# Loading the output projection in rows of 16, 8 and 4 KB, with attention outputs spread to match by mask products

## The chip, the cores and the metric

The kernel runs on one core of one Trainium2 chip. The metric is device time in microseconds (us) of that core, median over runs. Repeats of one kernel on one chip lie within about 0.5 us of each other.

PE is the matmul engine, DVE the vector engine, ACT the scalar engine, SP the engine that issues the loads. A load is one DMA instruction; 16 DMA engines work on it, each moving *packets*, here one contiguous run of bytes into one partition of SBUF, the core's on-chip memory, which has 128 partitions. A load *lands* when its bytes have arrived; each DMA engine reports the landing of its own share. The *cast* is the last arithmetic step, just before the store of the result.

## The reference, cut to what matters

```python
# one query token; 32 heads, 8 K/V groups of 4 heads, 65,536 keys, head size 128, bf16
xn = layernorm(x)
q  = (xn @ wq).reshape(32, 128)
o  = softmax(q @ K.T / sqrt(128)) @ V            # per head; K and V are 128 MiB each
out = x + o.reshape(4096) @ wo + ffn(xn)         # wo: 4096 x 512, 4 MiB
```

Every byte of K and V is used once, so 280.5 MB have to come in. wo is 1.5% of that, but it comes last.

## The kernel before

K comes in chunks of 4 MB (32 KB to a partition), V in chunks of 4 or 8 MB, all from one queue. PE transposes K, computes scores, and multiplies by V. wo has room only when the K buffers are free for good, so it is loaded last, behind the last half of V. The output of a head lies as a column: `oT_all[d, h]`, with the head's dimension d on the partitions.

A row of wo is 512 numbers, 1 KB. Four consecutive rows are put into one partition, so that a packet is 4 KB; the outputs must then be rearranged so that partition p holds the outputs for its four rows. That is done by 16 small matmuls with strided columns of the identity. Only the last group, whose outputs come last, keeps rows of 1 KB and needs no rearranging.

```python
WG = (4, GE - 4)            # GE = 7 groups, in two pieces
WH = (HPG - 1, 1)           # the last group: three heads, then one
def dma_wo():
    for i, n in enumerate(WG):
        ... dma(out=wo_sb[:, g0:g0+n], in_=A_wo[...].rearrange("(g p r) n -> p g (r n)", p=128, r=4))
    for i, n in enumerate(WH):
        cuts = ((0, 128),) if n > 1 else ((0, 120), (120, 128))   # last head in two loads
        for p0, p1 in cuts: ... dma(out=wl_sb[p0:p1, h0:h0+n, :], ...)
# ... after the last weighted sum:
weigh_3(GE, G, "oL")                      # outputs of the last group
for r in range(4):
    for h in range(4):
        matmul(pA[32*h:32*h+32, ...], lhsT=ident_bf[:, r:128:4], rhs=oT_all[:, h:28:4])
tensor_copy(oX_bf, pA[...])
# then, into one PSUM tile, 4 matmuls (one per 128 output columns) for each row block:
#   7 groups x 4 rows x 4 = 112 matmuls on oX_bf, then 4 heads x 4 = 16 on oT_all, cast, store
# ... (cut)
```

## Time and profile before

| | before |
|---|---|
| time, median of 3 runs | 658.9 us (658.89 to 658.99) |
| moved / mean rate | 280.65 MB / 427 GB/s |
| last landing of V, first and last DMA engine | 641.8 / 643.8 us |
| last landing: groups 0-3 / groups 4-6 / three heads / last head | 648.97 / 653.06 / 653.99 / 654.45 us |
| final cast starts | 655.03 us |

The first lines come from the page of the kernel before: busy tenths of the DMA engines in 40 equal slices of the span, the GB/s in the same slices, the packets by size, the main queue (packets, MB, share), and the shares of the chain of waits that ended last.

```profile
DMA  9999999999999999999999999999999999999997
GB/s 367 430 450 417 434 427 435 439 423 463 405 445 431 427 455 407 439 425 451 433 421 437 427 459 403 435 447 419 451 419 435 427 431 447 421 445 423 429 435 274
DMA packets 9277, 280.65 MB, mean 427 GB/s; under 512 B 1073, under 2 KB 1587, under 8 KB 2483
...
q1 hardware_dynamic: 9119, 280.50, 99.2%
...
DMA 65%; PE 33%; issue 1%; DVE 0%; SPq 0%
```

The DMA engines are at nine tenths or more in every slice but the last: the kernel is bound by the stream of bytes. The Trainium skill, "DMA: Bandwidth & Descriptors", section Specifications, gives a fabric ceiling of 435 GB/s and an HBM limit of about 358 GB/s per core (716 GB/s for a stack, divided by two cores); the 427 GB/s of the one core that runs here agree with the first and are above the second.

The end of the chain of waits (start in us, length in us, what), kernel before:

```profile
625.27 27.79 DMA kv<-in_A_wo_dram
653.06 0.04 issue
653.10 1.90 PE pss L786 x64
655.01 0.02 issue
655.03 0.29 DVE fin_bf L801
```

The timeline of PE at the end of the kernel before (start, length, line, output<-inputs, shapes, count; in brackets the idle time before it and what ended it):

```profile
648.55 0.31 PE L774 MATMUL pA<-oT_all,ident_bf 128*32 128x7 bf16 x16
648.71 0.60 PE L786 MATMUL pss<-f_rows,ones_f 128*1 128x128 f32 x8
649.60 1.88 PE L786 MATMUL pss<-kv,oX_bf 128*1 128x128 bf16 x64 [0.29 <-DVE oX_bf L778]
653.10 1.45 PE L786 MATMUL pss<-kv,oX_bf 128*1 128x128 bf16 x48 [1.63 <-DMA kv<-in_A_wo_dram]
654.34 0.64 PE L786 MATMUL pss<-kv,oT_all 128*1 128x128 bf16 x16
```

PE has the first four groups done by 651.5 us, waits for the second piece until 653.10, and then has 64 matmuls to go. They take 1.90 us and end after everything has landed.

### The profile page before, as it was taken

To read this page: it belongs to the slowest core of one execution; us is meant where nothing else is said; L and a number is where in the kernel's file an instruction comes from. 1 tells how busy PE (TensorE), PEld (TensorE's weight loads), DVE (VectorE), ACT (ScalarE), POOL (GpSimd) and SP (SyncE) were. 2 spreads that over 40 slices of the span, in tenths; PEclk is the share of its full clock that TensorE was granted. 3 is DMA by queue.
4 is the path that set the end of the run, shared out by engine and by line. 5 is a ranking of instruction groups with operands and counts; after the bars stand their busy time and mean duration, and the time that the engine had idled before them with its cause. 6 is when DMAs were issued, how large, how long until landed. Compare 5 with 4: busy or idle time off the path is not lost.

```text
span 657.4 us, 27984 instructions
## 1 busy us (share of the span) xinstructions
PE 539.8 (82%) x12695; PEld 512.5 (78%) x12695; DVE 273.8 (42%) x565; ACT 244.9 (37%) x454; POOL 2.9 (0%) x27
## 2 busy tenths in 40 slices
PE   2388799989789697878969787896978879697897
PEld 0187798978788696878969787895978779597886
DVE  3144162625436171453516345261634526154352
ACT  0134162524425162352505335160443516144351
POOL 0000000000000000000000000000000000000000
PEclk9688596967869596786958778595877959588695
DMA  9999999999999999999999999999999999999997
GB/s 367 430 450 417 434 427 435 439 423 463 405 445 431 427 455 407 439 425 451 433 421 437 427 459 403 435 447 419 451 419 435 427 431 447 421 445 423 429 435 274
DMA packets 9277, 280.65 MB, mean 427 GB/s; under 512 B 1073, under 2 KB 1587, under 8 KB 2483
## 3 DMA queue, kind: packets, MB, share of 16 engines
q1 hardware_dynamic: 9119, 280.50, 99.2%
q8 instruction: 8, 0.13, 0.1%
q10 hardware_dynamic: 148, 0.01, 0.0%
q14 instruction: 2, 0.02, 0.0%
HBM read 280.50 MB, written 0.00 MB: 427 GB/s over the span
## 4 chain that ended last, share of the span: by engine, by line
DMA 65%; PE 33%; issue 1%; DVE 0%; SPq 0%
DMA kv<-in_A_k_cache_dram 61%; PE pst L585 26%; DMA kv<-in_A_wo_dram 4%; PE pss L605 4%; PE pO L676 2%; PE pss L786 0%; PE pA L632 0%; PE pA L643 0%; DVE pmax L613 0%; PE pA L692 0%; DVE gmax L634 0%; DVE diag L636 0%; SPq L460 0%; SPq L453 0%; SPq L457 0%
## 5 line engine op out<-in xcount | busy, mean ns | idle before, releaser
L585 PE MATMUL pst<-ident_bf,kv 128*128 128x128 bf16 x4096 | 284.5, 236 | 34.8 <-DMA kv<-in_A_k_cache_dram 34.7
L595 ACT ACTIVATE kt_ring<-pst 128x1024 bf16<-128x1024 bf16 x192 | 195.6, 1027 | 311.7 <-PE pst L585 310.3
L585 PEld LDWEIGHTS pst<-ident_bf,kv 128*128 128x128 bf16 x4096 | 266.2, 107 | 43.1 <-DMA kv<-in_A_k_cache_dram 36.2
L593 DVE COPY kt_ring<-pst 128x1024 bf16<-128x1024 bf16 x320 | 210.8, 687 | 123.4 <-PE pst L585 121.0
L676 PE MATMUL pO<-P_bf,kv 128*128 128x4 bf16 x4096 | 115.1, 166 | 36.5 <-DMA kv<-in_A_v_cache_dram 31.9
L676 PEld LDWEIGHTS pO<-P_bf,kv 128*128 128x128 bf16 x4096 | 113.6, 104 | 37.8 <-DMA kv<-in_A_v_cache_dram 33.0
L605 PE MATMUL pss<-q_cur,kt_ring 128*128 128x4 bf16 x4096 | 111.9, 164 | 3.8 <-issue 3.8
L605 PEld LDWEIGHTS pss<-q_cur,kt_ring 128*128 128x128 bf16 x4096 | 109.3, 96 | 3.9 <-issue 3.9
L654 ACT ACTIVATE P_bf<-pss,negm 128x128 bf16<-128x128 f32 x128 | 50.9, 547 | 67.3 <-DVE negm L646 67.3
L685 DVE COPY o_all<-pO 128x4 f32 (+1 forms) x32 | 5.2, 162 | 120.4 <-PE pO L676 120.4
L613 DVE TENSOR_REDUCE pmax<-pss 128x4 f32<-128x512 f32 x32 | 22.1, 692 | 67.6 <-PE pss L605 67.6
L654 ACT ACTIVATION_READ_ACCUMULATOR P_bf<-pss,negm 128x1 f32 x128 | 35.3, 276 | 0.0
L643 PEld LDWEIGHTS pA<-diag,ones_f 4*128 4x128 f32 x64 | 12.6, 245 | 17.8 <-DVE diag L636 16.1
L632 PE MATMUL pA<-ident_f,pmax 128*4 128x128 f32 x64 | 13.9, 304 | 12.6 <-DVE pmax L613 12.6
L643 PE MATMUL pA<-diag,ones_f 4*128 4x4 f32 x64 | 15.4, 309 | 10.0 <-DVE diag L636 10.0
L632 PEld LDWEIGHTS pA<-ident_f,pmax 128*4 128x4 f32 x64 | 2.9, 84 | 15.8 <-DVE pmax L613 14.0
L634 DVE TENSOR_REDUCE gmax<-pA 4x1 f32<-4x128 f32 x32 | 8.8, 274 | 9.0 <-PE pA L632 9.0
L668 DVE COPY sums_all<-sums 128x8 f32 (+1 forms) x16 | 2.7, 172 | 23.4 <-ACT P_bf L654 23.4
L692 PE MATMUL pA<-sums_all,ones_f 128*128 128x128 f32 x32 | 12.4, 491 | 0.0
L646 DVE TENSOR_SCALAR negm<-pA 128x4 f32<-128x4 f32 x32 | 5.1, 161 | 10.8 <-PE pA L643 10.8
L692 PEld LDWEIGHTS pA<-sums_all,ones_f 128*128 128x128 f32 x32 | 8.0, 312 | 0.0
L636 DVE TENSOR_SCALAR diag<-ident_f,gmax 4x4 f32<-4x4 f32 x32 | 7.0, 217 | 1.1
(75 smaller groups left out, 47.4 us busy)
## 6 DMA issues: line engine op xcount, KB each, us to landing
kv<-in_A_k_cache_dram SPq DMA_DIRECT2D x32, 4096.0 KB, 27.5
kv<-in_A_v_cache_dram SPq DMA_DIRECT2D x4, 4096.0 KB, 24.2
kv<-in_A_wq_dram SPq DMA_DIRECT2D x1, 4096.0 KB, 12.3
kv<-in_B_w_dram SPq DMA_DIRECT2D x2, 1792.0 KB, 18.0
kv<-in_A_wo_dram SPq DMA_DIRECT2D x1, 2048.0 KB, 24.1
kv<-in_A_wo_dram SPq DMA_DIRECT2D x1, 1536.0 KB, 27.8
kv<-in_A_wo_dram SPq DMA_DIRECT2D x1, 384.0 KB, 17.8
kv<-in_A_v_cache_dram SPq DMA_DIRECT2D x14, 31.1
```

The costliest lines, as they stand in the source:

```text
L585: lambda tb=tb, at=at, b=b, tt=s * TPB + t: pe.transpose(pst[tb][:, at * 128:(at + 1) * 128], slot[b][:, tt, :], ident_bf[:, :]),
L593: e, fn = DVE, lambda tb=tb, dst=dst: dve.tensor_copy(out=dst, in_=pst[tb][:, :])
L595: e, fn = ACT, lambda tb=tb, dst=dst: act.activation(out=dst, in_=pst[tb][:, :], func=ACTF.Copy)
L605: lambda k=k, kb=kb, at=at, t=t: pe.matmul(pss[k][:, at:at + HPG], lhsT=kt_ring[:, kb * BCOL + t * 128:kb * BCOL + (t + 1) * 128], rhs=q_c ...
L613: lambda k=k: dve.tensor_reduce(out=pmax[:, :], in_=pss[k][:, 0:CW].rearrange("p (t j) -> p j t", j=HPG), axis=AX.X, op=ALU.max),
L632: sch.op(PE, lambda: pe.matmul(pA[0:HPG, PA_ST:PA_ST + 128], lhsT=pmax[:, 0:HPG], rhs=ident_f[:, :], start=True, stop=True), reads=["pmax" ...
L634: sch.op(DVE, lambda: dve.tensor_reduce(out=gmax4[:, :], in_=pA[0:HPG, PA_ST:PA_ST + 128], axis=AX.X, op=ALU.max), reads=["pA"], writes=[" ...
L636: sch.op(DVE, lambda: dve.tensor_scalar(out=diag4[:, :], in0=ident_f[0:HPG, 0:HPG], scalar1=gmax4[0:HPG, 0:1], scalar2=None, op0=ALU.mult) ...
L643: sch.op(PE, lambda: pe.matmul(pA[:, PA_SB:PA_SB + HPG], lhsT=ones_f[0:HPG, 0:128], rhs=diag4[0:HPG, 0:HPG], start=True, stop=True), reads ...
L654: lambda k=k, at=at, j=j, src=src: act.activation(out=P_v[k][:, :, j], in_=src[:, :, j], func=ACTF.Exp, bias=negm[:, at:at + 1], scale=1.0 ...
L676: lambda k=k, t=t: pe.matmul(pO[:, 0:HPG], lhsT=vslot[:, k * TPD + t, :], rhs=P_v[k][:, t, :], start=t == 0, stop=t == TPD - 1),
L692: sch.op(PE, lambda: pe.matmul(pA[:, PA_SUM:PA_SUM + NC], lhsT=ones_f[:, :], rhs=sums_all[:, :], start=True, stop=True), reads=["ones_f", ...
```

## The change

The intent: fewer and larger packets for wo, and less left to do after the last one. The seven groups load in pieces of four, two and one group. In a piece of n groups each partition gets 4n consecutive rows, so a packet is 16, 8 or 4 KB. To bring the outputs to these rows, DVE multiplies the outputs of a piece by a mask (1 where d // r equals the block), and one matmul per piece with a second mask (1 where d % r equals the column) puts each output on its partition. Six reduces over the identity make the masks, once, before the main loop. The last head's load is no longer cut in two.

```diff
+    WP = []                                   # becomes [(0, 4), (4, 2), (6, 1)]
+    while g0 < GE:
+        n = next(m for m in (4, 2, 1) if g0 + m <= GE)
+        WP.append((g0, n)); g0 += n
 def dma_wo():
-        for i, n in enumerate(WG):
-                in_=A_wo[...].rearrange("(g p r) n -> p g (r n)", p=128, r=HPG)
+        for i, (g0, n) in enumerate(WP):
+            r = n * HPG
+                in_=A_wo[...].rearrange("(p r) n -> p r n", r=r)
-            cuts = ((0, 128),) if n > 1 else ((0, 120), (120, 128))
+            # one load of 128 rows for the three heads, one for the last
+    def spread():                             # in the last pass, before its last weighted sum
+        for i, (g0, n) in enumerate(WP):
+            dve.tensor_tensor(out=oM_bf[:, i, :], in0=oT_all[...] broadcast, in1=part_m[i] broadcast, op=mult)
...
+    for i, (_, n) in enumerate(WP):           # before the loop: the masks
+        for t, pat in ((part_m[i], "p (a r) -> p a r"), (part_r[i], "p (a r) -> p r a")):
+            dve.tensor_reduce(out=t, in_=ident_f.rearrange(pat, r=r), op=max)
...
+    for i, (g0, n) in enumerate(WP):
+        pe.matmul(pA[...], lhsT=oM_bf[:, i, :], rhs=part_r[i])
+    dve.tensor_copy(out=oX_bf, in_=pA[...])
     weigh_3(GE, G, "oL")
-    for r in range(HPG):
-        for h in range(HPG):
-            pe.matmul(pA[32*h:32*h+32, ...], lhsT=ident_bf[:, r:128:HPG], rhs=oT_all[:, h:GE*HPG:HPG])
-    dve.tensor_copy(out=oX_bf, in_=pA[...])
... (cut: names, semaphores, indices of the final matmuls)
```

## The prediction

> **What bounds the kernel now.** The DMA stream. The page gives 280.65 MB at a mean of 427 GB/s and a DMA busy share of 9 in every slice but the last; the chain that ended last is 65% DMA. The Trainium skill, "DMA: Bandwidth & Descriptors", section Specifications, gives a fabric ceiling of 435 GB/s; this trace is 2% under it. So only three things can change: how efficiently wo's 4 MB move, what PE has to do after the last bytes, and the prologue.
>
> **The end (us from the start).** Landing records of the trace: the last V half lands at 641.8 on the first DMA engine and 643.84 on the last (seven engines run about 2 us late). wo follows on the same queue: first four groups by 648.97, other three by 653.06, three heads of the last group 653.99, last head 654.45. The timeline has PE waiting for wo until 653.10, then 64 matmuls at 30 ns spacing, ending about 655.0; DVE's final cast starts 655.03; the span ends at 657.4. Had PE followed the last landing at once, the cast could start near 654.9: PE's own backlog costs only about 0.1 us.
>
> **What the change does.**
> 1. wo packets. Packet records: 32 KB 1218 ns, 14 KB 535, 4 KB 164, 1 KB 46 to 60. Before, each engine moves 56 packets of 4 KB: 8.9 us (early engines) to 9.2 us (late ones), by landings. After: 8 each of 16, 8 and 4 KB. Estimate from neighbouring sizes: 8 x (609 + 307 + 162 ns) = 8.6 us. Saved: 0.35 to 0.6 us, on the critical path, because the late engines end the stream.
> 2. The last head's load is one DMA of 128 rows instead of 120 + 8: one 1 KB packet (0.05 us) less on some engines, eight more on one. About -0.05 to -0.1 us.
> 3. The group piece that lands last is now one group: 16 matmuls, not 48. PE's backlog (0.1 us) goes; PE then follows the last landing with four matmuls.
> 4. Spreading: 16 matmuls (0.31 us) become 3, and DVE gets 3 mask products (about 0.2 to 0.3 us each, from neighbouring operations on 128x112 and 128x128) at about 647.1 to 647.9, where it idles until 648.66. oX comes about 0.5 us earlier, but PE waits for wo anyway: worth nothing.
> 5. Six DVE reduces (about 0.38 us each, as one on 128x128 in the trace) fall at 26.3 to 28.6. DVE idles there until 33.76, PE until the first K chunk at 32.69: free.
>
> **Sum.** -0.5 -0.1 -0.1 gives about -0.7 us, all in the last 15 us. Predicted 658.2 us, eight times in ten between 657.7 and 658.7. Faster by over 2%: 0.005; within 2%: 0.99; slower by over 2%: 0.005.
>
> **What would show it.** Right: the last head's landing moves from 654.45 to about 653.8; 4 KB packets fall from 896 to 128, with 128 of 16 KB near 610 ns and 128 of 8 KB near 307; the cast starts near 654.3, and the chain ends DMA, a handful of matmuls, cast, output; PE's first K chunk stays at 32.69. Wrong: 16 KB rows no faster per byte than 4 KB ones, or PE busy well after the last landing.
>
> **What could make it wrong.** Instruction fetches on the DMA engines: each 16 KB block took 1.0 to 1.2 us of one engine, one of them at 651.65, within the tail. The added and removed instructions shift where blocks end; one fetch more, or one on a late engine, gives back the whole gain. The late engines' lag of 2 us may change. A sum this small is near the spread between chips.

## The result

The changed kernel took 658.34 us (median of 6 runs, 658.19 to 658.52), the kernel before 658.98 us beside it (6 runs, 658.89 to 659.32). The ratio is 0.9989, with a 95% interval of 0.9977 to 1.0002: the same, by the 2% mark. Ratios here are the mean time of one kernel's fast runs over that of the other's of the same rounds, so not quite the ratio of the medians. The interval touches 1, but no run of the changed kernel is as slow as the fastest run before, and the same kernel gave 0.9989 again (below). So about 0.64 us (by medians) to 0.70 us (by means) are gained.

The same page lines of the changed kernel (its slices differ little from those before):

```profile
DMA packets 8774, 280.65 MB, mean 427 GB/s; under 512 B 1082, under 2 KB 1596, under 8 KB 1724
...
q1 hardware_dynamic: 8616, 280.50, 99.2%
...
DMA 63%; PE 34%; issue 2%; DVE 0%; SPq 0%
```

There are 503 packets fewer for the same bytes, and the mean rate over the span is the same to three digits: the change concerns the last 12 us only. The end of its chain of waits:

```profile
636.99 16.42 DMA kv<-in_A_wo_dram
653.41 0.14 issue
653.55 0.63 PE pss L805 x13
654.17 0.02 issue
654.20 0.29 DVE fin_bf L820
```

Before, 64 matmuls stood between the last releasing load and the cast; now the 16 of the last group do (the chain takes up 13 of them; the timeline below has all 16). It begins the cast at 654.20 instead of 655.03 us. PE's timeline at the end of the changed kernel, and after it that of a second profile of the same kernel (the control run c1 below), which has PE's pieces unmerged:

```profile
649.11 0.22 PE L795 MATMUL pA<-part_r,oM_bf 128*128 128x16 bf16 x3
649.26 0.61 PE L805 MATMUL pss<-f_rows,ones_f 128*1 128x128 f32 x8
649.64 3.41 PE L805 MATMUL pss<-kv,oX_bf 128*1 128x128 bf16 x112
653.55 0.59 PE L805 MATMUL pss<-kv,oT_all 128*1 128x128 bf16 x16 [0.50 <-DMA kv<-in_A_wo_dram]
```

```profile
648.79 1.90 PE L805 MATMUL pss<-kv,oX_bf 128*1 128x128 bf16 x64
651.19 1.02 PE L805 MATMUL pss<-kv,oX_bf 128*1 128x128 bf16 x32 [0.50 <-DMA kv<-in_A_wo_dram]
652.47 0.60 PE L805 MATMUL pss<-kv,oX_bf 128*1 128x128 bf16 x16 [0.26 <-DMA kv<-in_A_wo_dram]
653.57 0.59 PE L805 MATMUL pss<-kv,oT_all 128*1 128x128 bf16 x16 [0.50 <-DMA kv<-in_A_wo_dram]
```

PE now follows each landing: four groups, two, one, the last group's heads. Its last wait for wo, as the list of waits between 645 and 657 us has it (engine, line, what it waited for, us in total, times, longest), before and after:

```profile
PE pss L786 <- DMA kv<-in_A_wo_dram: 1.6, 1, 1.6
```

```profile
PE pss L805 <- DMA kv<-in_A_wo_dram: 0.5, 1, 0.5
```

What I worked out from the landing records of the traces, which have one entry for each DMA engine of a load. The time for the groups runs from the last engine's landing of V to its landing of the last group:

```
us                                     before    changed
V, last half: first / last engine      641.8 / 643.84   641.7 / 643.76
groups of wo landed, last engine       653.06    652.41
  time for the groups, last engine       9.22      8.65
three heads landed                     653.99    653.41
last head landed                       654.45    653.73
cast                                   655.03    654.20
```

The last landing is 0.72 us earlier, the cast 0.83. A little of this comes from earlier in the kernel: V itself landed 0.08 us earlier, and the profiled run before took 659.17 us, 0.27 more than its kernel's median of 658.9. Counted from V's last landing, the last head lands 0.64 us earlier and the cast starts 0.75 us earlier. The new work is where the prediction put it. The instructions on the mask product in the changed kernel (durations in ns, least, median, most; first and last start):

```profile
L732 DVE TENSOR_TENSOR oM_bf<-oT_all,part_m x3: 283/284/292, 647.8 to 648.2; 128x128 bf16<-128x128 bf16 x3
...
L795 PE MATMUL pA<-part_r,oM_bf x3: 166/168/174, 649.1 to 649.2; 128*128 128x16 bf16 x1, 128*128 128x8 bf16 x1, 128*128 128x4 bf16 x1
```

The three products run while PE is still on the weighted sums and end before it needs them.

### The profile page after: what moved, and what is told of

It is laid out like the page before. It is cut to its first block, busy times and chain, and to the rows that moved or that the text cites. A ratio compares the mean times of both kernels' runs of the same rounds, so it can differ in the third digit from the quotient of the medians.

```text
span 656.5 us, 27968 instructions
## 1 busy us (share of the span) xinstructions
PE 539.3 (82%) x12682; PEld 512.1 (78%) x12682; DVE 275.7 (42%) x574; ACT 244.9 (37%) x454; POOL 2.9 (0%) x27
## 4 chain that ended last, share of the span: by engine, by line
DMA 63%; PE 34%; issue 2%; DVE 0%; SPq 0%
DMA kv<-in_A_k_cache_dram 61%; PE pst L590 27%; PE pss L610 4%; DMA kv<-in_A_wo_dram 3%; PE pO L681 2%; PE pA L637 0%; PE pA L648 0%; DVE pmax L618 0%; PE pA L697 0%; PE pss L805 0%; DVE gmax L639 0%; DVE diag L641 0%; SPq L470 0%; SPq L467 0%; SPq L463 0%
```

## The experiments

Twelve kernels ran, in three calls, each call on one chip with nine runs of the kernel before beside it. Each timed kernel ran five times. "Difference" is the mean of the kernel's runs less the mean of the runs before. Single runs of one kernel spread with a standard deviation of 0.04 to 0.22 us, so a difference of two means has a standard error of up to 0.13 us, and a difference of 0.1 us shows nothing by itself. All the intervals of the ratios are about 0.0013 wide to each side, too wide to separate these kernels from the kernel before or from each other; the exception is the run with 1 KB rows. What follows rests on the means together with the traces.

| run | median us | ratio | difference us |
|---|---|---|---|
| e1 before, one load for the last head | 658.89 | 0.9998 | -0.17 |
| e5 before, pieces of four, two, one group | 658.85 | 0.9998 | -0.12 |
| e2 changed, all rows 4 KB | 658.59 | 0.9994 | -0.44 |
| e4 changed, all rows 1 KB | 660.12 | 1.0018 | +1.13 |
| e3 changed, last head cut 120 + 8 | 658.58 | 0.9994 | -0.36 |
| e9 changed, last head cut 112 + 16 | 658.51 | 0.9992 | -0.54 |
| e10 changed, last head cut in columns | 658.42 | 0.9990 | -0.65 |
| e6 changed, big piece last | 658.99 | 0.9998 | -0.12 |
| e7 changed, masks three times | 658.28 | 0.9989 | -0.76 |
| e8 changed, rows to early engines | 658.69 | 0.9995 | -0.35 |
| c1 changed, again | 658.27 | 0.9989 | -0.69 |
| p1 changed, probe (one look) | 660.24 | | |

My theory after the result was that of the prediction: most of the gain from the size of the packets, a little from the head's load and from PE's backlog. The rivals were that one of the two small terms carries it, or the earlier outputs.

### c1: the changed kernel again

> The changed kernel once more, unchanged, so that the pieces run beside it on one chip. Expected 0.6 to 0.7 us under the kernel before, ratio 0.9989 to 0.9991; last landing near 653.7 us, last cast near 654.2 us.

No edit. 658.27 us, -0.69 us; last landing 653.75, cast 654.21. It repeats, on another chip.

### e2 and e4: the packet size alone

e2 makes seven pieces of one group, so each packet is 4 KB again (and there are seven mask products instead of three); everything else stays as changed.

```diff
-        n = next(m for m in (4, 2, 1) if g0 + m <= GE)
+        n = 1
```

> The changed kernel, but the seven groups load as seven pieces of one group, in rows of 4 KB: only the packet size goes back. Theory: 896 packets of 4 KB again, wo takes about 9.1 us on the late DMA engines instead of 8.65, the last head lands 0.4 to 0.6 us later than in the changed kernel, and the time is 0.4 to 0.6 us over it, so -0.1 to -0.3 us against the kernel before. Rival B (small last piece, and so less matmul work after it, carries the gain): as fast as the changed kernel, -0.6 us against before.

It came out at -0.44 us, so 0.25 us behind the changed kernel's -0.69. It was run at another time. The groups' time on the last engine was 8.96 us (643.83 to 652.79) against 8.66 in c1. So the packet size is worth 0.25 to 0.3 us: real, and half of what I had foreseen. This already said that the two small terms are not small.

One thing was not held fixed, the clock granted to PE at the end. In the profiled runs of e2 and e9 it was 1.00 from about 652 us until after the cast, and the last matmuls took 217 ns each; in the other profiles it was 0.50, and they took 311 to 314 ns (c1). The cast followed the last landing after 0.32 us in e2 and 0.33 in e9, after 0.46 us in c1. So the times of e2 and e9 may flatter them by up to 0.14 us, and the landings are the safer measure: counted from V's last landing, the last head landed after 10.25 us in e2 and 9.98 in c1, 0.27 us apart.

e4 goes the other way: every head in rows of 1 KB, as the last group has them, which needs no spreading at all.

```diff
-   in_=A_wo[...].rearrange("(p r) n -> p r n", r=r)
+   in_=A_wo[...].rearrange("(r p) n -> p r n", r=r)
-   (masks, mask products, spreading matmuls, copy)
-   fin_mm(kt, oX_bf[:, r:r + 1], ...)
+   fin_mm(kt, oT_all[:, r:r + 1], ...)
```

> The changed kernel with all heads of wo in rows of 1 KB, so that no spreading, no masks and no extra copy are needed: the suspected cost made larger. Theory: each engine moves 256 packets of 1 KB at 47 to 50 ns, 12.0 to 12.8 us, against 10.2 us in the changed kernel: +1.9 to +2.6 us over it, +1.2 to +2.0 us over the kernel before. Rival C (getting rid of the 16 spreading matmuls and having the outputs ready earlier matters): at least as fast as the changed kernel.

+1.13 us (a little under the 1.2 to 2.0 expected), 1.8 us over the changed kernel: the groups' time on the last engine was 10.48 us. The rival, that doing without the rearranging pays, is out. Minimum packet times in the traces are 46 ns for 1 KB, 159 for 4 KB, 309 for 8 KB, 611 for 16 KB and 2418 for 64 KB. At the rate of the 64 KB packets (27.1 bytes per ns) 1 KB would need 38 and 4 KB 151 ns, so each small packet costs about 8 ns on top. That is enough to account for the gain of large rows here: 32 fewer packets per engine (56 to 24) times 8 ns are 0.26 us.

### e5 and e6: what PE still has to do

e5 is the kernel before with its 4 KB rows in pieces of four, two and one group.

```diff
-    WG = (4, GE - 4)
+    WG = (4, 2, 1)
```

> The kernel before, with its seven groups in pieces of four, two and one, still in rows of 4 KB and with its own spreading: only the matmul work after the last group piece goes down, from 48 to 16. The prediction's step 3 says 0.1 us; the difference of the 4 KB run and the run with one head load says 0.25 us. Expected -0.1 to -0.3 us against before; the last cast then comes 0.3 to 0.5 us after the last landing, where the run with one head load had 0.67. Rival (packet size is all): no change.

-0.12 us. PE's timeline in e5:

```profile
649.06 1.87 PE L786 MATMUL pss<-kv,oX_bf 128*1 128x128 bf16 x64 [0.39 <-DMA kv<-in_A_wo_dram]
651.52 1.02 PE L786 MATMUL pss<-kv,oX_bf 128*1 128x128 bf16 x32 [0.59 <-DMA kv<-in_A_wo_dram]
652.99 0.60 PE L786 MATMUL pss<-kv,oX_bf 128*1 128x128 bf16 x16 [0.44 <-DMA kv<-in_A_wo_dram]
654.01 0.59 PE L786 MATMUL pss<-kv,oT_all 128*1 128x128 bf16 x16 [0.42 <-DMA kv<-in_A_wo_dram]
```

PE waits before each piece, as in the changed kernel, and the cast came 0.45 us after the last landing (654.66 and 654.21). By the runs the step is as large as the prediction had it, but -0.12 with a standard error of 0.10 is not clear of the spread. By the profiles it is larger: counted from V's last landing the cast starts after 10.86 us instead of 11.19.

e6 is the changed kernel with the pieces in the reverse order: the same packets, but the largest piece lands last.

```diff
-        n = next(m for m in (4, 2, 1) if g0 + m <= GE)
+        n = (1, 2, 4)[len(WP)]
```

> The changed kernel with its three pieces in the order one, two, four groups: the same packets, but 64 matmuls after the last piece instead of 16. Theory: PE's backlog binds again: from that piece's landing near 652.4 us, 80 matmuls at 27 to 30 ns put the last cast near 654.9 us, 0.6 to 0.9 us over the changed kernel, so about level with the kernel before. Rival (only the DMA stream counts): as fast as the changed kernel, -0.7 us.

-0.12 us: of the changed kernel's gain 0.57 us are gone (against c1; 0.64 against e7 below). Everything landed as in c1 (last head 653.77), but the end of the chain of waits reads:

```profile
625.95 26.51 DMA kv<-in_A_wo_dram
652.46 0.04 issue
652.50 2.33 PE pss L805 x80
...
654.86 0.29 DVE fin_bf L820
```

80 matmuls after the piece's landing at 652.46 us put the cast at 654.86. So in this kernel the large rows pay only if the piece that lands last is small.

### e1 and e3: the last head's load

e1 is the kernel before with the last head as one load; e3 is the changed kernel with the head cut as before.

```diff
# e1
-            cuts = ((0, 128),) if n > 1 else ((0, 120), (120, 128))
+            cuts = ((0, 128),)
# e3: the reverse, in the changed kernel
```

> The kernel before, with only the last head's load made one DMA of 128 rows. Theory (the gain is mostly packet size): last landing of the head moves from 654.45 to about 654.35 us, but PE still works off 64 matmuls after the last group piece lands at 653.06, so the final cast stays at about 655.0 and the time moves by 0 to -0.1 us. Rival A (the merged head load carries the gain): -0.5 us or more, ratio at most 0.9992.

> The changed kernel, with the last head's load cut again into 120 and 8 rows. The one-DMA load alone gave the kernel before 0.2 us where 0.05 to 0.1 was foreseen. Theory 2 (the 120 rows spare the highest engine, which the probe shows to be an early one, and the 8 rows go to the eight lowest, two of which are late): 0.1 to 0.25 us slower than the changed kernel, last landing 0.1 to 0.15 us later. Rival (the 0.2 us were chance): no difference.

e1 gave -0.17 us, where I expected 0 to -0.1; and in its trace not only the head but the groups before it landed earlier than in the kernel before (652.71 instead of 653.06 us; 0.13 of this because V landed earlier, 0.22 counted from V's landing), which my reasoning did not allow for: the groups are loaded *ahead* of the head. e3 gave -0.36, so it loses 0.33 us (standard error 0.10) of the changed kernel's gain, more than the 0.1 to 0.25 expected. Part of that is not the head's: in e3's profile V landed 0.12 us later than in c1, and counted from V's landing the last head came 0.14 us and the cast 0.22 us later.

### p1: which engines are late

In all traces seven of the 16 engines end the stream late, the last of them 1.8 to 2.1 us behind the first engine, with two engines in between. The probe loads the last head as sixteen loads of 8, 1, 2, ... 15 rows, each with its own semaphore.

```diff
-            one load of 128 rows for the last head
+        for i, k in enumerate((8,) + tuple(range(1, 16))):     # 8 + 120 rows
+            dma(out=wl_sb[p0:p0 + k, 3:4, :], ..., psem[i]); p0 += k
```

> A look, not a timing: the last head's 128 rows load as sixteen DMAs of 8, 1, 2, ... 15 rows, each on its own semaphore. If a DMA of k rows runs on the k lowest engines, the landing records tell which engines are the late ones (2 us behind). If the late ones follow the instruction fetches in order, they should be neighbours; if every engine of one half is late, the last bytes could be put on the other half. The time should be 0.2 to 0.6 us over the changed kernel, for the lowest engine carries 16 rows instead of 8.

The Trainium skill, "DMA: Bandwidth & Descriptors", section "Why a DMA increments its semaphore by 16 and not by 1", says that a load runs on the largest number k of engines up to 16 that divides its rows, that these are the lowest-numbered k, and that the issuer writes the other 16 - k counts at once. The records agree: each load of k rows has one early record and k later ones. Comparing each list with the one before it gives, for each of the engines 0 to 14, when it was free, and engine 15 by elimination: 0, 2, 4, 7, 8, 10 and 15 were early, 5, 6, 9, 11, 12, 13 and 14 late, 1 and 3 between. So the cut into 120 and 8 rows spared engine 15, which was early, and gave one more row to engines 5 and 6, which were late. That was theory 2. It accounts for one or two rows, 0.05 to 0.1 us, and not for 0.33. The probe itself was far slower than expected (660.24 us): each tiny load took 0.17 to 0.20 us of an engine where its packet takes 0.05.

### e9 and e10: why the cut costs more than its packets

In the packet records something else stands out. These are mean durations of the packets that started between 651.5 and 652.0 us, when the early engines work on the last head while others still move 4 KB packets of groups or 1 KB packets of the three heads (the 1 KB column also holds the last head's own):

```
                           4 KB: ns (count)    1 KB: ns
before  (120 + 8 rows)       195 (20)            56.5
e1      (128 rows)           163 (20)            50.3
changed (128 rows)           164 (6)             46.7
c1      (128 rows)           167 (5)             47.5
e3      (120 + 8 rows)       204 (6)             59.5
e5      (120 + 8 rows)       173 (18)            50.9
e9      (112 + 16 rows)      196 (8)             56.0
e10     (2 x 128 half rows)  166 (9)             47.3
e8      (95 + 32 + 1 rows)   242 (12)            72.1
```

While a cut load is under way, the packets of *other* loads slow down by about a fifth or more. e5 is no exception: its slow stretch only comes later, 651.8 to 652.3 us, with 203 ns (6 packets) and 60 ns. In e8, where the narrow loads come right behind the groups, it begins at 650.4 us instead of 651.5 as in e3: the slow stretch moves with the narrow load. The other engine traffic in this stretch, a fetch of 16 KB of instructions, isn't the cause: in e3 and e9 it began at 652.36 and 652.34 us, after the slow stretch had set in, and e1, e2 and e7 had it at 651.96, 652.00 and 652.15 without one.

Theory 3 is shared SBUF ports. The Trainium skill, "DMA: Bandwidth & Descriptors", section "The descriptor swizzle", says that in a transfer to 128 partitions each engine writes the partitions of one SBUF port. My inference: a load of 120 or 8 rows is dealt out differently, so an engine would then write into ports that belong to others. e9 cuts the head into 112 and 16 rows, both on all 16 engines in equal shares; e10 cuts it by columns, two loads of all 128 partitions.

```diff
# e9, to e3
-            cuts = ... ((0, 120), (120, 128))
+            cuts = ... ((0, 112), (112, 128))
# e10, to e3
-                    out=wl_sb[p0:p1, h0:h0 + n, :]                    # rows
+                    out=wl_sb[:, h0:h0 + n, p0:p1]                    # columns 0:256, 256:512
```

> The changed kernel with the last head's load cut into 112 and 16 rows instead of 120 and 8. Both run on all 16 engines with equal shares (7 rows and 1), so no engine is spared and none gets more. Theory 3 (SBUF ports shared: in a load that isn't 128 partitions wide an engine no longer has its own port, as the skill's page on DMA has it for the full load, and packets of other engines in flight slow down): 4 KB packets of the late engines rise from 162 to 190 ns or more from 651.5 us on, as with 120 and 8; 0.2 to 0.4 us slower than the changed kernel. Theory 2 (engine 15 spared for nothing, extra rows on late engines 5 and 6): packets stay at 162 and 47 ns, at most 0.1 us slower.

> The changed kernel with the last head's load as two DMAs of all 128 rows, each with half the columns (512 B packets): two DMAs, but full width. Theory 3 (shared ports): the late engines' 4 KB packets stay near 162 ns. A rival theory 4 (a second small DMA as such disturbs the others): they rise as with 120 and 8. Its own packets are smaller: 16 of 512 B instead of 8 of 1 KB, 0 to 0.4 us more at the end, so the time alone decides little here.

e9 slowed the others as the cut into 120 and 8 did (196 ns), though its engines have equal shares; e10, also two loads, did not (166 ns), though it has twice the packets. So neither the spared engine (theory 2) nor a second load as such (theory 4) is the cause; a load that isn't 128 partitions wide is. How strong the effect is differs: the probe's sixteen tiny loads brought 4 KB packets only to 174 ns (10 packets). By time, e9 was 0.15 us behind c1 and 0.22 behind e7 (0.2 to 0.4 were expected, and PE's clock helped e9, see e2; its last head landed 0.28 us later than c1's, counted from V); e10 was 0.04 and 0.11 us behind them, which is within the spread. That the sharing happens at the ports is my inference from the skill's picture, and the runs fit it; no run here shows a port. The width of a load also changes which rows of wo each engine reads, and no run separates the reading side from the writing side.

### e7: the masks

```diff
-    for i, (_, n) in enumerate(WP):
+    for i, (_, n) in list(enumerate(WP)) * 3:
```

> The changed kernel with its six mask reduces done three times over (18 instead of 6): the suspected cost in the prologue tripled. Six took 1.5 us of DVE time from 25.9 us on, so 18 end near 30.5 us, before the first PSUM copy at 33.6 us. Expected: no change from the changed kernel, -0.7 us against before; the first matmul for K stays at 32.5 us. If the masks had cost something, 3 us more of them would show 0.3 us or more.

-0.76 us, no slower than the changed kernel. First DVE around the masks in the changed kernel, then in e7 the last mask, PE's first matmul on K, and the first copy of DVE:

```profile
25.31 0.69 DVE L580 COPY f_rows<-pO 128x512 f32<-128x512 f32 x1 [2.29 <-PE pO L525]
25.92 0.27 DVE L781 TENSOR_REDUCE part_m<-ident_f 128x8 bf16<-128x128 f32 x1
...
27.05 0.36 DVE L781 TENSOR_REDUCE part_r<-ident_f 128x4 bf16<-128x128 f32 x1
33.59 0.69 DVE L598 COPY kt_ring<-pst 128x1024 bf16<-128x1024 bf16 x1 [6.17 <-PE pst L590]
```

```profile
29.05 0.37 DVE L781 TENSOR_REDUCE part_r<-ident_f 128x4 bf16<-128x128 f32 x1
...
32.82 3.49 PE L590 MATMUL pst<-ident_bf,kv 128*128 128x128 bf16 x31 [8.39 <-DMA kv<-in_A_k_cache_dram]
33.89 0.69 DVE L598 COPY kt_ring<-pst 128x1024 bf16<-128x1024 bf16 x1 [4.47 <-PE pst L590]
```

Even 18 reduces end 3.4 us before PE gets its first K chunk, and the idle time before PE's first matmul is a wait for that chunk. The masks are free.

### e8: a try at a better version

If late engines end the stream, the last bytes should go to early ones. e8 loads one head of the last group as 95 rows (on engines 0 to 4), 32 rows and 1 row.

```diff
-    WH = (HPG - 1, 1)
+    WH = (1, 2, 1)
+            cuts = (0, 95, 127, 128) if i == 0 else (0, 128)
```

> A try at a better version. In the probe engines 0, 2 and 4 were early and 1 and 3 about 0.9 us ahead of the late ones. The changed kernel, but the last group's heads load as one, two and one, and the first of them as three DMAs of 95, 32 and 1 rows, of which 95 should run on engines 0 to 4 alone (19 rows each) and 32 on all. Late engines get 6 rows of 1 KB less, at 47 ns: last landing about 0.28 us earlier, and time 0.15 to 0.3 us under the changed kernel. If the fixed cost of more DMAs (0.12 us each in the probe) lands on the late engines, or engines 1 and 3 become the late ones, nothing is gained.

It failed: -0.35 us, 0.34 us slower than the changed kernel; last landing 653.90 against 653.75 (0.32 us later, counted from V's landing). The 95-row load gave the late engines less, and slowed everything in flight (242 ns instead of 163 to 167 for 4 KB). It ran before I had theory 3, and is the largest case of it. No run here beats the changed kernel beyond the spread.

## Why the prediction was right or wrong

The total was right: 658.2 us foreseen, within 657.7 to 658.7, and 658.34 measured; -0.7 foreseen, -0.64 by medians and -0.69 to -0.70 by means. Its parts were not. The calls allow this path from the kernel before to the changed one, all in one call. Beside the times stands the same step by the profiles: the start of the cast, counted from V's last landing, which leaves out what differed earlier in the kernel (before 11.19, e5 10.86, e3 10.66, c1 10.44 us; PE's clock was 0.50 at the end in all four):

```
step                                       us by runs    by profiles  foreseen
before -> e5   small last piece           -0.12 +- 0.10    -0.33      -0.1
e5 -> e3       larger rows, new spreading -0.24 +- 0.13    -0.20      -0.5
e3 -> c1       last head in one load      -0.33 +- 0.10    -0.22      -0.05 to -0.1
sum                                       -0.69 +- 0.05    -0.75      -0.7
```

The +- is one standard error. The changed kernel, c1 and e7, which have the same end, all start the cast 10.44 us after V's landing; the other kernels of the path have one profile each. The two columns share the gain out differently, but in both the large rows carry half or less of what was foreseen, and the two small terms carry the rest. How much each of those two is worth is not settled.

- **Step 1, packets ("saved: 0.35 to 0.6 us", -0.5 in the sum): mis-sized.** It measured -0.24 to -0.25 by time and 0.3 us by landings. The 8.65 us after were foreseen closely (8.6). What was wrong was the baseline: I took the 9.2 us of the late engines as what 4 KB packets cost, though 163 ns x 56 is 9.1, and the mean of 164.4 ns already held packets of 195 ns. With the head in one load the same packets took 9.0 us (e1: 643.71 to 652.71; e2: 8.96), so 0.22 to 0.26 of the 0.57 us between 9.22 and 8.65 belong to the cut load and not to the packet size.
- **Step 2, one head load ("about -0.05 to -0.1 us"): mis-sized, and its mechanism was incomplete.** It measured -0.17 in the kernel before and -0.33 in the changed one. I counted the packets of the load itself; what it did to the packets of others was not in the sum. The two errors cancelled: the slowed packets stood in the baseline of step 1, and step 2 took them away without my knowing. That the total came out right was in this part luck, and it does not vouch for the reasoning.
- **Step 3, backlog (-0.1): right as to the wait, its size open.** -0.12 by e5's runs and -0.33 by its profile; PE's last four matmuls now wait for the last landing (653.73), their first weight load beginning at 653.77. e6 shows what the order of the pieces is worth: about 0.6 us.
- **Step 4, spreading off the path: right.** The mask products took 0.28 us each at 647.75 to 648.45, before PE was done. The outputs came not 0.5 us earlier on the clock, since PE ended its weighted sums 0.6 us later in that profile, but about 0.6 us sooner after the weighted sum; PE waits for wo in either case.
- **Step 5, masks free: right.** They took 0.27 to 0.37 us each and 1.5 us together, in idle time; three times as many changed nothing.
- **The feared instruction fetch** moved from 651.65 to 652.23 us and no loss from it can be seen.

What stays open: whether it is SBUF ports that the cut loads share, or something on the reading side, and how the gain divides between the head's load and the small last piece. The cost of the cut came out at 0.17 us in the kernel before, 0.33 in the changed one and 0.15 for the other cut; by the cast counted from V's landing it is 0.22 (e1), 0.22 (e3) and 0.15 us (e9, at the higher clock), so the spread of the runs allows one cost for all.

## What to carry to other kernels

In a stream that keeps all DMA engines busy, make loads full 128 partitions wide: here a small load cut by partitions slowed the loads ahead of it, and that cost more than its own packets. Large rows saved about 8 ns a packet here, which pays only where there are many packets per engine, and the piece that lands last should be small, or the matmuls after it eat the gain. When a sum of small terms comes out right, undo the terms one by one before believing them.

## What the Trainium skill lacked or had wrong

- "DMA: Bandwidth & Descriptors", sections "The descriptor swizzle" and "Rules for kernel authors": the swizzle is given for 128 partitions, and the rule on two transfers to disjoint partition halves says "Don't bother — they serialize". Lacking is that a narrower load slows other loads in flight: 4 KB packets took 195 to 204 ns instead of 163 beside 120 + 8 or 112 + 16 rows, 242 ns beside 95 + 32 + 1 rows, and 166 ns beside two loads of 128 rows.
- The same page, "Why small descriptors are slow (HBM only)", has its packet overhead worked out for 256 bytes. The runs show about 8 ns for each packet of 1 and of 4 KB, so going from 56 packets of 4 KB to 24 of 4 to 16 KB per engine was still worth 0.25 to 0.3 us.
- That page has no figure for the time of an engine that each of many queued tiny loads takes: here loads of 1 to 15 rows took an engine 0.17 to 0.20 us each, where the 1 KB packet takes 0.05.
- "Runtime: NRT & Kernel Launch", section "Instruction fetch mechanics", calls the fetch hidden behind instruction issue, which is about the engine that issues. It lacks what the fetch may do to a saturated DMA stream: the number of DMA engines that land 1.3 us or more after the first grows with the 16 KB fetches in the trace before (4 late engines at 60 us, 5 at 70, 6 at 79, 7 from 89 us on; the fetches began at 28, 45, 53, 60, 68, 74 and 82 us), and the lag of about 2 us stays to the end of the kernel. That is a count that fits, and no run took a fetch away.
